# Key-value products of batches 3 to 7: two heads in the column halves of the TensorE array instead of a masked 128x128 product

## The chip, the cores and the metric

The kernel runs on one core of one Trainium2 chip. The metric is the device time of one launch in microseconds (us). Before the change, three runs gave 277.59, 277.82 and 278.0 us, a median of 277.82 us. Engines are named as in the profile: PE is TensorE's matmul, PEld its weight load, DVE is VectorE, ACT is ScalarE, POOL is GpSimd and SP is SyncE, which here only issues DMAs.

## What is computed

The kernel is a linear attention without softmax, followed by a feed-forward layer with a leaky activation:

```
kv  = einsum('bhsd,bhse->bhde', k, v)        # 64 x 64 for each batch and head
o   = einsum('bhsd,bhde->bhse', q, kv)
x   = o / sqrt(mean(o*o, -1) + 1e-6) * g_norm  # then heads side by side: 4608 x 512
h   = x @ w_in                                # 4608 x 2048
g   = max(h, 0) + alpha * min(h, 0)
out = g @ w_out                               # 4608 x 512, float32
```

There are 8 batches, 8 heads, 576 positions in each, 64 columns in each head, d_model 512 and d_ff 2048. Inputs and output are float32; the matrix products run on float16 operands and add up in float32.

## The kernel before, in words

**Windows and units.** The 4608 rows are worked in 9 windows of 512 rows (`w`). A window of the feed-forward part has 16 units (`u`), one for each block of 128 columns of the hidden layer. In unit `u` of window `w`, PE runs four matmuls with 512 moving columns into one PSUM bank (`m1_mm`, line 487; from window 3 on the first unit is cut into 384 and 128 columns, line 510), ACT and DVE turn that bank into 128 x 512 of the hidden layer (`m1_evac`, lines 494 and 498), and PE runs seven matmuls with 256 moving columns (`prod_mm`, line 665) of the product with `w_out` of window `w - 1`, which is done with 7 products of half size in place of 8. The sums for that are DVE's (`s_sum`, lines 603 to 609), and so are most of the reads of the finished sums (`y_read`, lines 697 to 709).

**Attention between the units.** After these matmuls, the call `attention(w + 1, u)` puts a piece of the next window's attention into the same unit. The order of the instructions of every engine is the order of the program (a manual schedule on all five engines), so the tables `ATT_ROW`, `QT_AT`, `REG_AT` and `REG_2` say in which unit a piece is issued. For windows 3 to 8 the pieces are these:

- `kv`: `row_kv` calls `step_kv` for each of the four pairs of heads. Heads 2j and 2j+1 are loaded side by side, so `k` and `v` of a pair have 128 columns. Five matmuls (four runs of 128 rows and one rest, lines 351 to 358) add up the 128x128 product of the whole pair in PSUM. Its two diagonal blocks of 64x64 are the products that are wanted; the other two blocks mix two heads. DVE's `tensor_mul` with `mask32` (line 360) writes the tile `kv_sb` in float16, with zeros in the mixed blocks. Pairs 0 and 2 use the PSUM bank with tag `s`, pairs 1 and 3 one of the two with tag `o`. Two pairs are issued in unit 0 and two in unit 1 (in units 2 and 3 for batch 3).
- `mm`: `rows_mm` multiplies 128 rows of `q` (transposed, in `qt_sb`) with `kv_sb` of the four pairs, with 128 moving columns (lines 429, 435 and 439), and ACT squares the result (line 444). It comes in units 2, 4, 6 and 8 (4, 5, 7 and 9 for window 3), the third time into the bank with tag `s`.
- `ssq`, `rs`, `norm`: DVE's sums (line 450), ACT's root (line 459), DVE's product (line 467), and a transposing DMA that SP issues.

**Loads.** POOL issues loads that cast to float16 (`load_gated`). `k` of a later batch lands in `kst` with the heads outermost, and ACT copies it pair by pair to `ksb` (`regroup_pair`, line 177): in units 9, 11, 13 and 15 of the window before (`REG_AT`), for batch 3 in units 0, 0, 1 and 2 of window 2 (`REG_2`). `v` is read by the matmuls as it landed (`vst`, the rest in `vsb`).

Batches 0 to 2 make their products with `step_kv` too, at other places: batch 0 in the start phase, batches 1 and 2 during windows 0 and 1.

Of the kernel before, what the change touches and what calls it, by code (L numbers as in the profile page):

```python
# [9 lines left out]
FP32 = mybir.dt.float32  # L10
FP16 = mybir.dt.float16
# [6 lines left out]
def kernel(  # L18
# [11 lines left out]
    nc = tc.nc  # L30

    B, H, S, D = q.shape
# [3 lines left out]
    P = 128  # L36
    NPAIR = H // 2
    W = 512
# [15 lines left out]
    const_p = ctx.enter_context(tc.tile_pool(name="constp", bufs=1))  # L54
# [4 lines left out]
    attn_p = ctx.enter_context(tc.tile_pool(name="attn", bufs=2))  # L59
# [6 lines left out]
    ps_s = ctx.enter_context(tc.tile_pool(name="pss", bufs=1, space=bass.MemoryType.PSUM))  # L66
# [10 lines left out]
    def early_pair(eng, nm, tag):  # L77
# [14 lines left out]
            name=nc.get_next_instruction_name(),  # L92
# [9 lines left out]
    mask32 = const_p.tile([P, P], FP32, name="mask32")  # L102
# [8 lines left out]
    qt_sb = [const_p.tile([P, NPAIR, PAD + S + PAD], FP16, name=f"qt_sb{i}") for i in range(2)]  # L111
# [6 lines left out]
    for r in range(P // D):  # L118
        nc.sync.dma_start(
            out=alpha_row[NF : NF + 1, r * D : (r + 1) * D], in_=g_norm[:].unsqueeze(0)  # L120
# [7 lines left out]
    for i in range(NBUF):  # L128
        t = {}
# [34 lines left out]
    def buf_of(b, nm):  # L164
        return bufs[min(b, B_NAT) % 2 if nm == "q" else b % NBUF][nm]
# [38 lines left out]
    def regroup_pair(b, nm, j):  # L204
        regroup(b, nm, 2 * j, 2 * j + 2, nc.scalar)
# [76 lines left out]


    qts, kvs, xts = {}, {}, {}

    def rows(b):
        return P0 if b == 0 else P

    def n_runs(b):
        return T0 if b == 0 else NT  # L290

    def pair_cols(b, nm, j):
        def f(t):
            n = rows(b)
            if nm == "v" and b == 0:
                h = 2 * j % HH
                return stages[b, nm, 2 * j // HH][0:n, h : h + 2, t, :]
            if nm == "v" and t < TPP:
                return stages[b, nm][:, 2 * j : 2 * j + 2, t, :]
            if nm == "v":  # L300
                return buf_of(b, nm)[0:n, 0, 2 * j : 2 * j + 2, :]
            return buf_of(b, nm)[0:n, t, 2 * j : 2 * j + 2, :]
        return f
# [33 lines left out]
    def dma_t(b, ts=tuple(range(NT))):  # L337
        qt = qt_sb[b % 2][:, :, PAD : PAD + S]
        for t in ts:
            c0, c1 = t * P, min((t + 1) * P, S)  # L340
            src = stages[b, "q"][:, t] if t < TPP else buf_of(b, "q")[0:REM, TPP]
            nc.sync.dma_start_transpose(
                out=qt[:, :, c0:c1], in_=src.rearrange("p h d -> p (h d)"),
            )
        for j in range(NPAIR):
            qts[b, j] = qt_sb[b % 2][:, j, PAD : PAD + S]

    def step_kv(b, j, pool=(ps_s, "s")):
        ks, vs = pair_cols(b, "k", j), pair_cols(b, "v", j)
        kv_ps = pool[0].tile([P, P], FP32, name="kv_ps", tag=pool[1])  # L350
        for t in range(n_runs(b)):
            nc.tensor.matmul(  # L352
                out=kv_ps[:],
                lhsT=ks(t),
                rhs=vs(t),
                start=(t == 0),
                stop=(t == n_runs(b) - 1),
            )
        kvs[b, j] = attn_p.tile([P, P], FP16, name="kv_sb", tag=f"kv{j}")
        nc.vector.tensor_mul(out=kvs[b, j][:], in0=kv_ps[:], in1=mask32[:])  # L360


    ots = {}
# [1 line left out]
    def step_ot(w, j, pool=None, parts=1):  # L365
        if pool is not None:
            ot_ps = pool[0].tile([P, W], FP32, name="ot_ps", tag=pool[1])
        else:
            ot_ps = ps_o.tile([P, W], FP32, name="ot_ps", tag="o")
        n0 = w * W  # L370
        while n0 < (w + 1) * W:
            b = n0 // S
            n1 = min((b + 1) * S, (w + 1) * W, n0 + W // parts)
            nc.tensor.matmul(  # L374
                out=ot_ps[:, n0 - w * W : n1 - w * W], lhsT=kvs[b, j][:],
                rhs=qts[b, j][:, n0 - b * S : n1 - b * S], start=True, stop=True,
            )
            n0 = n1
        sq = attn_p.tile([P, W], FP16, name="sq_sb")
        for c in col_parts(parts):  # L380
            nc.scalar.activation(out=sq[:, c], in_=ot_ps[:, c], func=AF.Square)
        ots[w, j] = (ot_ps, sq)

    def col_parts(parts):
        n = W // parts
        return [slice(i * n, (i + 1) * n) for i in range(parts)]
# [33 lines left out]
    def rows_mm(w, i):  # L420
        n0 = w * W + i * P
        b, r = divmod(n0, S)
        pool, tag = (ps_s, "s") if i == 2 else (ps_o, "o")
        o_ps = pool.tile([P, W], FP32, name="or_ps", tag=tag)
        for j in range(NPAIR):
            cols = o_ps[:, j * P : (j + 1) * P]
            if r + P <= S:
                c = PAD + r
                nc.tensor.matmul(  # L429
                    out=cols, lhsT=qt_sb[b % 2][:, j, c : c + P], rhs=kvs[b, j][:],  # L430
                    start=True, stop=True,
                )
            else:
                assert r + PAD == S
                nc.tensor.matmul(
                    out=cols, lhsT=qt_sb[b % 2][:, j, S : S + P], rhs=kvs[b, j][:],
                    start=True, stop=False,
                )
                nc.tensor.matmul(
                    out=cols, lhsT=qt_sb[(b + 1) % 2][:, j, 0:P], rhs=kvs[b + 1, j][:],  # L440
                    start=False, stop=True,
                )
        sq = attn_p.tile([P, W], FP16, name="sq_sb")
        nc.scalar.activation(out=sq[:], in_=o_ps[:], func=AF.Square)  # L444
        ots[w, "r", i] = (o_ps, sq)
# [291 lines left out]
    Q_POOL, S_POOL, O_POOL = (ps_q, "q"), (ps_s, "s"), (ps_o, "o")  # L737
# [7 lines left out]
    def h_at(i):  # L745
# [7 lines left out]
        out=alpha_ps[:], lhsT=alpha_row[0 : NF + 1, 0:P], rhs=ident[0 : NF + 1, 0 : NF + 1],  # L753
# [6 lines left out]
        out=beta_sb[:], in0=alpha_ps[:, 0:NF], scalar1=-1.0, scalar2=1.0, op0=ALU.mult, op1=ALU.add,  # L760
    )
    keep_warm(2)
    step_kv(0, 0)
    keep_warm(1)
    step_ot(0, 0)
    regroup0("q", 1)
    keep_warm(1)
    step_t(0, 1, h_at(1))
    regroup0("k", 1)
    ssq_mm(0, 0)  # L770
    keep_warm(1)
    step_kv(0, 1, h_at(2))
    keep_warm(1)
    step_ot(0, 1)
    regroup0("q", 2, 2)
    keep_warm(1)
# [20 lines left out]
    first = [ps_h.tile([P, W], FP32, name="h_ps", tag="h1")]  # L797
# [170 lines left out]
            ATT_1.setdefault(at, []).append((what, j))  # L968
    ATT = {"t": step_t, "kv": step_kv, "ot": step_ot, "ssq": step_ssq}

    def row_kv(w, j):
        step_kv(w, j, O_POOL if j % 2 else S_POOL)

    ATT_ROW = {}
    for first, kv_at, d in ((True, (2, 2, 3, 3), 1), (False, (0, 0, 1, 1), 0)):
        at_row = {}
        for what, ats in (
            ("kv", kv_at), ("mm", (2 + d, 4, 6, 8)), ("ssq", (4, 6, 8, 10)),
            ("rs", (5, 7, 9, 11)), ("norm", (5, 7, 9, 11)),
        ):  # L980
            for j, at in enumerate(ats):
                at_row.setdefault(at if what == "kv" else at + d, []).append((what, j))
        ATT_ROW[first] = at_row
    ROWS = {"kv": row_kv, "mm": rows_mm, "ssq": rows_ssq, "rs": rows_rs, "norm": rows_norm}
    QT_AT = {False: {7: (0,), 9: (1,), 11: (2, 3, 4)}, True: {8: (0,), 10: (1,), 12: (2, 3, 4)}}

    def attention(w, u):
        if W_ROW <= w < NW:
            for what, j in ATT_ROW[w == W_ROW].get(u, ()):
                if what != "kv" or w < B:  # L990
                    ROWS[what](w, j)
            if w + 1 < B:
                dma_t(w + 1, QT_AT[w == W_ROW].get(u, ()))
        elif w < NW:
            for what, j in (ATT_1 if w == 2 else ATT_AT).get(u, ()):
                if what == "t" and w >= B_NAT:
                    continue
                if w < B or what in ("ot", "ssq"):
                    if w == 2 and what in ("kv", "ssq"):
                        pool = Q_POOL if j % 2 == 0 else S_POOL  # L1000
                        (step_kv if what == "kv" else step_ssq)(w, j, pool)
                    else:
                        ATT[what](w, j)
# [1 line left out]
    REG_AT = {9 + 2 * j: (("k", j),) for j in range(NPAIR)}  # L1005

    Y3_AT = [(13, 13), (13, 13), (13, 13), (13, 14), (14, 14), (14, 15), (15, 15), (15, 15), (15, 15), (15, 15), (15, 15), (15, 15), (15, 15), (15, 15), (15, 16), (16, 16)]
    REG_2 = {0: (("k", 0), ("k", 1)), 1: (("k", 2),), 2: (("k", 3),)}

    for w in range(1, NW):  # L1010
        if w + 2 < B:
            load_gated(w + 2)
        for u in range(NF):
# [45 lines left out]
            if w == 2:  # L1059
                for nm, j in REG_2.get(u, ()):  # L1060
                    regroup_pair(3, nm, j)
    w = NW - 1
# [16 lines left out]
    for h in range(2):  # L1079
        half = slice(h * P, (h + 1) * P)  # L1080
        for n, i in Y_LIST[-NK:]:
# [3 lines left out]
            out=y_sb[:, 1, half], in0=ybank[w, "Z", 1 + h][:, half], in1=part[w, "u2"][:, 1, half]  # L1085
# [33 lines left out]
```

## Time and profile before

| what | value |
|---|---|
| median of three runs | 277.82 us (277.59 to 278.0) |
| profiled execution: span from its first to its last instruction | 275.2 us |
| what lies around the span (277.82 less 275.2) | 2.6 us |
| granted TensorE clock, mean | 1.000 |
| PE busy | 269.1 us, 1973 matmuls |
| PEld busy | 176.1 us, 1973 weight loads |
| DVE busy | 231.2 us, 451 instructions |
| ACT busy | 154.9 us, 286 instructions |
| POOL busy | 86.3 us, 123 instructions |

The profiled execution is known by its span; the difference to the median stands for what lies before its first and after its last instruction. A line of a group gives the source line, engine, operation, tiles and shapes, how often it ran, then busy time and the mean of one in ns, then idle time before it. Matmuls are pipelined: a matmul is shown as busy until its last result is out, so consecutive ones overlap in the records, and the time that one takes from the engine is the distance to the start of the next. The chain of work that ended last is therefore the better view of PE; its pieces give start, length and count.

### The profile page before, as it was taken

To read this page: it belongs to the slowest core of one execution; us is meant where nothing else is said; L and a number is where in the kernel's file an instruction comes from. 1 tells how busy PE (TensorE), PEld (TensorE's weight loads), DVE (VectorE), ACT (ScalarE), POOL (GpSimd) and SP (SyncE) were. 2 spreads that over 40 slices of the span, in tenths; PEclk is the share of its full clock that TensorE was granted. 3 is DMA by queue.
4 is the path that set the end of the run, shared out by engine and by line. 5 is a ranking of instruction groups with operands and counts; after the bars stand their busy time and mean duration, and the time that the engine had idled before them with its cause. 6 is when DMAs were issued, how large, how long until landed. Compare 5 with 4: busy or idle time off the path is not lost.

```text
span 275.2 us, 5282 instructions
## 1 busy us (share of the span) xinstructions
PE 269.1 (98%) x1973; PEld 176.1 (64%) x1973; DVE 231.2 (84%) x451; ACT 154.9 (56%) x286; POOL 86.3 (31%) x123
## 2 busy tenths in 40 slices
PE   7899999999999999999999999999999999999995
PEld 3454454555776776676667766676667666666794
DVE  6659758799789979997999799978997999887863
ACT  3568446799989746644665456645545553444210
POOL 8853463660912338127322641100111011000200
PEclk9999999999999999999999999999999999999999
DMA  8999999999999849997984799520322032201223
GB/s 160 197 203 198 197 202 189 215 132 182 129 172 129 124 91 138 174 204 100 173 155 120 114 166 175 118 87 2 76 76 79 6 83 67 76 2 38 72 84 114
DMA packets 87341, 34.53 MB, mean 125 GB/s; under 512 B 58884, under 2 KB 85652, under 8 KB 87316
## 3 DMA queue, kind: packets, MB, share of 16 engines
q0 software_dynamic: 58064, 24.35, 68.3%
q1 hardware_dynamic: 28212, 8.83, 16.9%
q10 hardware_dynamic: 1040, 1.02, 1.2%
q8 instruction: 15, 0.25, 0.4%
q14 instruction: 10, 0.08, 0.1%
HBM read 36.71 MB, written 9.44 MB: 168 GB/s over the span
## 4 chain that ended last, share of the span: by engine, by line
PE 87%; DMA 10%; POOL 1%; issue 1%; DVE 0%; POOLq 0%
PE h_ps L487 38%; PE yY L665 15%; PE yX L665 10%; PE yZ L665 10%; DMA qst<-in_q_dram 8%; PE y L519 4%; PE kv_ps L352 3%; DMA w_in_sb<-in_moe_w_in_dram 2%; PE h_ps L510 2%; PE or_ps L429 2%; PE qt_ps L308 1%; PE ssq_ps L397 1%; PE yZ L660 1%; PE ot_ps L374 1%; POOL vst L142 0%
## 5 line engine op out<-in xcount | busy, mean ns | idle before, releaser
L487 PE MATMUL h_ps<-xt,w_in_sb 128*128 128x512 f16 x544 | 136.8, 379 | 0.0
L494 ACT ACTIVATE m_sb<-h_ps 128x512 f32<-128x512 f32 x144 | 86.1, 598 | 79.8 <-PE h_ps L487 69.6
L498 DVE SCALAR_TENSOR_TENSOR gt<-m_sb,beta_sb,h_ps 128x512 f16<-128x512 f32 x144 | 106.4, 745 | 23.6 <-ACT m_sb L494 21.8
L487 PEld LDWEIGHTS <-w_in_sb 128*128 128x128 f16 x544 | 51.6, 98 | 38.9
L530 POOL DMA_DIRECT2D out_dram<-y_sb x36 | 22.6, 630 | 134.8 <-DVE y_sb L709 43.7
L665 PEld LDWEIGHTS <-s 128*128 128x128 f16 x496 | 48.5, 98 | 19.1
L665 PEld LDWEIGHTS <-gt 128*128 128x128 f16 x384 | 37.3, 98 | 14.0
L665 PE MATMUL yY<-wsum,s 128*128 128x256 f16 x256 | 36.3, 273 | 0.0
L665 PE MATMUL yX<-w_out_sb,gt 128*128 128x256 f16 x256 | 36.1, 273 | 0.0
L159 POOL DMA_DIRECT2D qst<-in_q_dram x20 | 17.7, 923 | 1.8 <-DMA vst<-in_v_dram 1.8
L665 PE MATMUL yY<-wsum,gt 128*128 128x256 f16 x128 | 17.6, 273 | 0.0
L444 ACT ACTIVATE sq_sb<-or_ps 128x512 f16<-128x512 f32 x24 | 14.3, 597 | 5.7 <-PE or_ps L429 4.6
L665 PE MATMUL yZ<-wsum,s 128*128 128x256 f16 x120 | 16.7, 273 | 0.0
L665 PE MATMUL yZ<-w_out_sb,s 128*128 128x256 f16 x120 | 16.7, 273 | 0.0
L467 DVE TENSOR_TENSOR x_rows<-or_ps,rstd_r 128x512 f16<-128x512 f32 x24 | 16.4, 685 | 0.0
L450 DVE TENSOR_REDUCE ssq_r<-sq_sb 128x8 f32<-128x512 f16 x24 | 16.3, 680 | 0.0
L519 PE MATMUL y<-w_out_sb,gt 128*128 128x512 f16 x64 | 15.9, 379 | 0.0
L605 DVE TENSOR_TENSOR s<-s,gt 128x512 f16<-128x512 f16 x32 | 13.5, 422 | 0.5
L603 DVE TENSOR_TENSOR s<-gt 128x512 f16<-128x512 f16 x32 | 13.5, 420 | 0.0
L609 DVE TENSOR_TENSOR s<-gt,s 128x512 f16<-128x512 f16 x32 | 13.3, 420 | 0.0
L697 DVE TENSOR_TENSOR u<-yY,p 128x512 f32<-128x512 f32 x16 | 11.0, 684 | 1.9 <-PE yY L665 1.7
L607 DVE TENSOR_TENSOR s<-gt 128x512 f16<-128x512 f16 x32 | 12.6, 418 | 0.0
(88 smaller groups left out, 269.9 us busy)
## 6 DMA issues: line engine op xcount, KB each, us to landing
out_dram<-y_sb POOLq DMA_DIRECT2D x16, 256.0 KB, 2.7
kst<-in_k_dram POOLq DMA_DIRECT2D x7, 512.0 KB, 7.0
vst<-in_v_dram POOLq DMA_DIRECT2D x6, 512.0 KB, 9.2
qst<-in_q_dram POOLq DMA_DIRECT2D x20, 128.0 KB, 6.8
w_out_sb<-in_moe_w_out_dram POOLq DMA_DIRECT2D x8, 256.0 KB, 11.6
out_dram<-y_sb SPq DMA_DIRECT2D x5, 256.0 KB, 2.3
w_in_sb<-in_moe_w_in_dram POOLq DMA_DIRECT2D x2, 512.0 KB, 10.6
qst<-in_q_dram POOLq DMA_DIRECT2D x2, 512.0 KB, 12.2
```

What stands on the lines that cost most here:

```text
L159: nc.gpsimd.dma_start(out=st[:, t, :, :], in_=srcs["q"][b, :, t * P : (t + 1) * P, :].rearrange("h p d -> p h d"),)
L444: nc.scalar.activation(out=sq[:], in_=o_ps[:], func=AF.Square)
L450: nc.vector.tensor_reduce(out=ssq[:], in_=sq[:].rearrange("p (h d) -> p h d", h=H), axis=mybir.AxisListType.X, op=ALU.add,)
L467: nc.vector.tensor_tensor(out=xr[:], in0=o_ps[:].rearrange("p (h d) -> p h d", h=H), in1=rstd[:].unsqueeze(2).to_broadcast([P, H, D]), op= ...
L487: nc.tensor.matmul(out=h_ps[:], lhsT=w_in_blk(c, g), rhs=xts[w][:, c, :], start=(c == 0), stop=(c == NC - 1),)
L494: nc.scalar.activation(out=m_sb[:], in_=h_ps[:], func=AF.Relu, scale=-1.0)
L498: nc.vector.scalar_tensor_tensor(out=gts[w, i][:, r, :], in0=m_sb[:], scalar=beta_sb[:, g : g + 1], in1=h_ps[:], op0=ALU.mult, op1=ALU.add,)
L519: nc.tensor.matmul(out=y[:], lhsT=gt_cols(w, g, a * P, (a + 1) * P), rhs=w_out_blk(g), start=(g == 0), stop=(g == NF - 1),)
L530: engs[store_turn[0] % len(engs)].dma_start(out=dst, in_=src)
L603: nc.vector.tensor_add(out=t[:], in0=a21, in1=a22)
L605: nc.vector.tensor_sub(out=t[:], in0=sums[w, 1, k][:], in1=a11)
L665: nc.tensor.matmul(out=bank, lhsT=lhs, rhs=rhs, start=fresh, stop=(c == NK - 1), skip_group_check=True,)
```

## The change

For batches 3 to 7, `row_kv` makes the products for each head by itself. The stationary operand is the 64 columns of `k` of one head, the moving operand the 64 columns of `v` of the same head. The even head's result goes to PSUM partitions 0 to 63 and the odd head's to partitions 64 to 127, so the two heads of a pair use the two column halves of the array, and their matmuls alternate. All four pairs share one PSUM tile of 128 x 256 in the bank with tag `s`. Two DVE copies, of 64 partitions x 256 elements each, move the diagonal blocks to float16. The results of a batch lie in one of two constant tiles `kv_masked`; `step_kv`, which batches 0 to 2 still use, writes all of its 128x128 there, zeros in the mixed blocks included, and later batches write only the diagonal blocks. All four pairs are issued in unit 0 (unit 2 for batch 3), and for batch 3 the copy of `k` of pair 3 moves from unit 2 to unit 1.

```diff
+    kv_masked = [const_p.tile([P, NPAIR, P], FP16, name=f"kv_masked{i}") for i in range(2)]
...
-        kvs[b, j] = attn_p.tile([P, P], FP16, name="kv_sb", tag=f"kv{j}")
-        nc.vector.tensor_mul(out=kvs[b, j][:], in0=kv_ps[:], in1=mask32[:])
+        kvs[b, j] = kv_masked[b % 2][:, j, :]
+        nc.vector.tensor_mul(out=kvs[b, j], in0=kv_ps[:], in1=mask32[:])
...
-    def row_kv(w, j):
-        step_kv(w, j, O_POOL if j % 2 else S_POOL)
+    def row_kv(b):
+        kv_ps = ps_s.tile([P, NPAIR, D], FP32, name="kv_ps", tag="s")
+        for j in range(NPAIR):
+            ks, vs = pair_cols(b, "k", j), pair_cols(b, "v", j)
+            for t in range(n_runs(b)):
+                for i in range(2):
+                    rows_i = slice(i * D, (i + 1) * D)
+                    nc.tensor.matmul(
+                        out=kv_ps[rows_i, j, :], lhsT=ks(t)[:, i, :], rhs=vs(t)[:, i, :],
+                        start=(t == 0), stop=(t == n_runs(b) - 1), skip_group_check=True,
+                    )
+        for i in range(2):
+            rows_i = slice(i * D, (i + 1) * D)
+            nc.vector.tensor_copy(
+                out=kv_masked[b % 2][rows_i, :, rows_i], in_=kv_ps[rows_i, :, :]
+            )
+        for j in range(NPAIR):
+            kvs[b, j] = kv_masked[b % 2][:, j, :]
...
-    for first, kv_at, d in ((True, (2, 2, 3, 3), 1), (False, (0, 0, 1, 1), 0)):
-        at_row = {}
+    for first, kv_at, d in ((True, 2, 1), (False, 0, 0)):
+        at_row = {kv_at: [("kv", None)]}
...
-    REG_2 = {0: (("k", 0), ("k", 1)), 1: (("k", 2),), 2: (("k", 3),)}
+    REG_2 = {0: (("k", 0), ("k", 1)), 1: (("k", 2), ("k", 3))}
```

The uses of `kvs[b, j]` in `step_ot` and `rows_mm` change only in that they take the slice as it is.

More of the change, by code (lines that the diff above doesn't have):

```diff
@@ L374, in step_ot @@
             nc.tensor.matmul(
-                out=ot_ps[:, n0 - w * W : n1 - w * W], lhsT=kvs[b, j][:],
+                out=ot_ps[:, n0 - w * W : n1 - w * W], lhsT=kvs[b, j],
                 rhs=qts[b, j][:, n0 - b * S : n1 - b * S], start=True, stop=True,
@@ L429, in rows_mm @@
                 nc.tensor.matmul(
-                    out=cols, lhsT=qt_sb[b % 2][:, j, c : c + P], rhs=kvs[b, j][:],
+                    out=cols, lhsT=qt_sb[b % 2][:, j, c : c + P], rhs=kvs[b, j],
                     start=True, stop=True,
@@ L435, in rows_mm @@
                 nc.tensor.matmul(
-                    out=cols, lhsT=qt_sb[b % 2][:, j, S : S + P], rhs=kvs[b, j][:],
+                    out=cols, lhsT=qt_sb[b % 2][:, j, S : S + P], rhs=kvs[b, j],
                     start=True, stop=False,
@@ L439, in rows_mm @@
                 nc.tensor.matmul(
-                    out=cols, lhsT=qt_sb[(b + 1) % 2][:, j, 0:P], rhs=kvs[b + 1, j][:],
+                    out=cols, lhsT=qt_sb[(b + 1) % 2][:, j, 0:P], rhs=kvs[b + 1, j],
                     start=False, stop=True,
@@ L969 @@
     ATT = {"t": step_t, "kv": step_kv, "ot": step_ot, "ssq": step_ssq}
-    def row_kv(w, j):
-        step_kv(w, j, O_POOL if j % 2 else S_POOL)
+    def row_kv(b):
[16 more added lines that the diff above has]
+            kvs[b, j] = kv_masked[b % 2][:, j, :]
     ATT_ROW = {}
-    for first, kv_at, d in ((True, (2, 2, 3, 3), 1), (False, (0, 0, 1, 1), 0)):
-        at_row = {}
+    for first, kv_at, d in ((True, 2, 1), (False, 0, 0)):
+        at_row = {kv_at: [("kv", None)]}
         for what, ats in (
-            ("kv", kv_at), ("mm", (2 + d, 4, 6, 8)), ("ssq", (4, 6, 8, 10)),
+            ("mm", (2 + d, 4, 6, 8)), ("ssq", (4, 6, 8, 10)),
             ("rs", (5, 7, 9, 11)), ("norm", (5, 7, 9, 11)),
@@ L981 @@
             for j, at in enumerate(ats):
-                at_row.setdefault(at if what == "kv" else at + d, []).append((what, j))
+                at_row.setdefault(at + d, []).append((what, j))
         ATT_ROW[first] = at_row
-    ROWS = {"kv": row_kv, "mm": rows_mm, "ssq": rows_ssq, "rs": rows_rs, "norm": rows_norm}
+    ROWS = {"mm": rows_mm, "ssq": rows_ssq, "rs": rows_rs, "norm": rows_norm}
     QT_AT = {False: {7: (0,), 9: (1,), 11: (2, 3, 4)}, True: {8: (0,), 10: (1,), 12: (2, 3, 4)}}
@@ L989, in attention @@
             for what, j in ATT_ROW[w == W_ROW].get(u, ()):
-                if what != "kv" or w < B:
+                if what != "kv":
                     ROWS[what](w, j)
+                elif w < B:
+                    row_kv(w)
             if w + 1 < B:
```

## The prediction

> **What bounds the kernel now.** I read the busy table first, then the chain of work that ended last, then that chain in the windows around the key-value products, because a mean over the whole span can't say what one stage is limited by.
>
> ```profile
> PE 269.1 (98%) x1973; PEld 176.1 (64%) x1973; DVE 231.2 (84%) x451; ACT 154.9 (56%) x286; POOL 86.3 (31%) x123
> ...
> PE 87%; DMA 10%; POOL 1%; issue 1%; DVE 0%; POOLq 0%
> ```
>
> PE is busy for 98% and holds 87% of the chain; the DMA part lies in the first 32 us, before batch 3 is touched. Matmul records overlap, so "98% busy" alone doesn't show that PE is full. The chain in order of time does (start, length, piece, number of matmuls), here around the products of batch 5 and, after the dots, of batch 6:
>
> ```profile
> 123.31 0.33 PE yX L665 x3
> 123.64 0.56 PE kv_ps L352 x10
> 124.20 0.86 PE h_ps L487 x4
> 125.06 0.76 PE yX L665 x7
> 125.83 0.56 PE kv_ps L352 x10
> 126.39 0.86 PE h_ps L487 x4
> ...
> 151.93 0.56 PE kv_ps L352 x10
> ```
>
> Each piece begins where the last one ends, and no other engine stands between. A unit is 0.86 + 0.77 = 1.63 us, 16 of them 26.06; with two kv pieces of 0.56 and four or_ps pieces of 0.22 a window should take 28.06 us. The kv blocks of batches 4 and 5 start at 95.58 and 123.64: 28.06 apart. From 123.64 to 151.93 it is 28.29, and there one or_ps piece is of eight matmuls, 0.22 more. So in these windows PE's stream of columns is the time, to the hundredth, and whatever the kv blocks gain or lose on PE goes into the total one for one.
>
> **The price of a matmul by its width.** Distances in the chain: 0.216 us at 512 columns (0.86 / 4), 0.1094 at 256 (1.75 for 16), 0.0556 at 128:
>
> ```profile
> 266.61 0.87 PE yZ L665 x8
> 267.49 0.89 PE yZ L660 x16
> ```
>
> That is 0.418 ns a column and 2 ns more. At 64 columns it makes 28.9 ns. The trace has 64-column matmuls (ot_ps, line 374) only in front of one of 448 columns; the two take 0.22 us together, as one of 512 does, so 64 columns with a weight load of their own cost their share there.
>
> **The change on PE.** It removes 20 matmuls of 128 columns per batch, 1.11 us, and adds 40 of 64 columns and 40 weight loads of 64 columns. Five batches have 5.56 us at stake, 2.0% of the span. The trace has no matmul on half of the array, so three things are unknown.
>
> (a) *Do the two halves run beside each other?* If so, 20 pairs at 28.9 ns take 0.58 us, 0.53 less. If one follows the other, 40 at 28.9 are 1.16, which is 0.05 more. These are the ends. I take the first: the two heads of a pair use different columns of the array, different output partitions and different operands, and nothing in the program orders them.
>
> (b) *Do the loads keep up?* A load is recorded with 98 ns, but loads overlap:
>
> ```profile
> 11.44 0.28 PEld L308 LDWEIGHTS <-qsb 96*128 96x128 f16 x6 [0.55 <-DVE qsb L199]
> ...
> 11.45 0.43 PE L308 MATMUL qt_ps<-ident,qsb 96*128 96x96 f16 x6
> ```
>
> Six loads of 128 columns in 0.28 us: (0.28 - 0.098) / 5 = 36 ns apart, under matmuls (0.43 - 0.21) / 5 = 44 ns apart. That is the densest that the trace shows, and the matmuls may set it, so it is an upper bound for a full load. A half load should then cost between nothing and 36 ns of PE's time; an estimate of 18 ns, half the columns at that pace, would be covered by matmuls run singly and nearly by pairs (2 x 18 against 29). I take nothing, since the 64-column matmuls above showed none; the outer end, a load that nothing hides, is the recorded 98 ns. If half loads follow each other at 36 ns, a block takes 40 x 0.036 = 1.44 us, 0.33 more than now.
>
> [...]
>
> (c) *What does going to halves and back cost?* Twice a batch. At most the pipeline runs empty: a 128-column matmul is recorded with 219 ns and the next normally starts after 56, so 0.163 us each. At least nothing. The nearest row is the one change of shape in the trace, the 17-row transposition of line 752:
>
> ```profile
> 5.85 0.66 PE L308 MATMUL qt_ps<-ident,qsb 96*128 96x96 f16 x6
> 6.44 0.28 PE L752 MATMUL alpha_ps<-ident,y_sb 17*128 17x17 f32 x1
> 6.66 0.83 PE L277 MATMUL warm_ps<-y_sb 128*128 128x512 f16 x2
> ```
>
> The six before it stand (0.66 - 0.28) / 5 = 76 ns apart, so the seventh was due about 6.31 and came at 6.44, before the six were out (6.51): 0.13 us late, at half the later pace (76 against 44 ns). I halve it: 0.07 us a change, 0.13 a block. [...]
>
> Block: 0.58 + 0.13 = 0.71 us in place of 1.11: 0.40 less, five times 2.0 us.
>
> **DVE.** Removed: four products of 128 columns, 286 ns each, 1.14 us. Added: two copies of 256 elements a partition. No such copy is in the trace; the nearest rows are
>
> ```profile
> L360 DVE TENSOR_TENSOR kv_sb<-kv_ps,mask 128x128 f16<-128x128 f32 x32 | 8.1, 286 | 3.4 <-PE kv_ps L352 3.4
> ...
> L713 DVE TENSOR_TENSOR y_sb<-yZ,u 128x256 f32<-128x256 f32 x2 | 0.8, 422 | 0.2 <-PE yZ L665 0.2
> ```
>
> so 286 to 422 ns each, 0.84 us by the upper: 0.3 a batch less. None of it is on the path. They queue ahead of the next gt (line 498): around batch 6 the products start at 153.24 and the next gt at 154.01, so 0.84 pushes it back by 0.07, and its bank is wanted one unit later. The reader of the new products is or_ps, two units on at the earliest. Were that cover gone, 0.1 a batch. Over a window DVE is busy for 25.5 of 28.1 us; with PE at 27.7 it stays under.
>
> **Order.** All four pairs now need `k` in unit 0. ACT's last copy (line 177) ran 150.06 to 150.67 and the block starts at 151.76: covered by 1.1 us. For batch 3 the copy of pair 3 moves from 72.04 to behind the one at 69.96, so to about 70.5 to 71.1, while the block starts at 70.56 and reaches pair 3 at 71.0: up to 0.1 us, once, and the m_sb queued behind it starts 0.5 later, one unit before its bank is wanted. No DMA is issued at another place in its queue; `v` comes free one unit earlier, which no load in these windows waits for. The shared bank `s` is next wanted by or_ps three units later; the banks `o` lose a user.
>
> **Sum.** 5 x 0.40 - 0.1 = 1.9 us off the span of 275.2, so 273.3, and with the 2.6 us around it (277.82 - 275.2) 275.9 us.
>
> **Rivals.** *Loads set the pace* (slower). Place: the 40 loads of a block. It decides as soon as half loads can't be hidden, follow each other and take over 28 ns (1.11 / 40). At 36 ns: 5 x 0.33 = +1.65, 279.5 us; with two full drains of 0.163 a block +1.6 more, 281.1. At 98 ns, nothing hidden, 5 x 2.8 = +14, 292. For it: twice the loads for half the time. Against: loads took 64% of PE's time and matmuls never waited for one in the windows.
> *The changes of shape eat the gain.* At 0.163 and with the first load of each side not hidden (0.098) a change costs 0.26, a block 0.58 + 0.52 = 1.10: no change, 277.8. Drains alone: 0.91, 276.8.
> *The change does not do what it says*: the halves follow each other. 1.16 + 0.13 a block, +0.9 us, 278.7; without a price for the changes of shape 278.1.
> *DVE takes the bound*: against it the 2.6 us that it idles in each window, against 0.4 that PE gives back.
>
> **How the numbers follow.** Pairs beside each other, loads hidden, price of the change of shape 0 to 0.163: 275.2 to 276.9, 0.50. Gain eaten or halves in turn without further price: 277.3 to 278.4, 0.16. Loads or halves in turn with a price: 278.4 to 281.1, 0.31, two thirds of it below 280; beyond 281.1, 0.03. Measurements of this kernel can tell about 0.2%, 0.56 us, from no change. Faster by more 0.51, within 0.15, slower by more 0.34. The range from 275.0 to 280.0 leaves out about 0.14. The likeliest case by itself is 275.2 to 276.9.
>
> **What would show it.** Right: the kv piece of the chain is one of 40 matmuls and 0.6 to 0.9 us long, windows are 27.7 us apart, the pieces on both sides touch it, DVE shows two copies below 0.43. Wrong: starts of kv matmuls 36 ns or more apart with loads back to back, a gap ahead of and behind the block, idle PE in the units after it, or a wait of kv for ksb in the window of batch 3.

## The result and the profile after

The changed kernel takes 276.48 us (median of 14 runs, 275.96 to 277.03) against 277.56 us for the kernel before beside it (14 runs, 276.63 to 278.0). The ratio is 0.9962, with a 95% interval of 0.9952 to 0.9971: 1.05 us faster, where 1.9 us were forecast.

The busy table of after comes first, then its chain of work (start, length, piece, number of matmuls) around the products of batches 4 and 5.

```profile
PE 267.8 (97%) x2073; PEld 173.5 (63%) x2073; DVE 230.8 (84%) x441; ACT 154.9 (56%) x286; POOL 87.0 (32%) x123
```

```profile
96.54 0.75 PE kv_ps L979 x40
...
124.01 0.33 PE yX L666 x3
124.34 0.75 PE kv_ps L979 x40
125.09 0.97 PE h_ps L488 x4
126.06 0.77 PE yX L666 x7
```

The 40 matmuls are one piece of 0.75 us in place of two of 0.56. But the four matmuls behind it take 0.97 in place of 0.86: 0.11 us are lost there, and the chain counts them to the next piece. So a block costs 0.75 + 0.11 = 0.86 against 1.11. The starts of the blocks confirm it: 96.54 to 124.34 is 27.80 us, where it was 28.06. Still no other engine stands in the chain here.

The span is 275.1 us, hardly less than the 275.2 of before, and this needs care. The first block of batch 3 starts at 71.49 in this execution and at 70.56 in that of before, 0.93 us later, and the delay comes from loads in the start phase: the two longest pieces that wait for q took 6.66 and 15.04 us against 6.05 and 14.73. In five other executions of kernels that are the same up to there it starts at 71.26 (even heads only), 70.85 (halves in turn), 70.64 (thirty-two moving columns), 70.88 (whole pairs) and 71.09 (the changed kernel again), so the start phase by itself varies by some 0.6 us from execution to execution. From the first block to the end it is 203.6 us (275.1 - 71.49) against 204.6 (275.2 - 70.56): 1.0 us less, which is what the runs show. This execution was the slowest of the 14.

Something else takes a little of the gain. In the first unit of window 4 the second group of four h_ps matmuls takes 0.32 us in this execution and 0.22 in that of before, so PE is 0.10 late there. In the profile of the same kernel run again (last experiment) it is 0.22 late at this place, and the chain names the wait, a transposing DMA that lands at 95.51:

```profile
91.90 3.61 DMA xt<-x_rows
...
95.55 0.38 PE h_ps L511 x4
```

None of the other eleven profiles shows it. Whether the change has a part in it isn't shown.

One instruction level down, these are after's matmuls around the block, then its weight loads:

```profile
123.85 0.49 PE L666 MATMUL yX<-w_out_sb,gt 128*128 128x256 f16 x3
124.27 0.32 PE L979 MATMUL kv_ps<-vst,ksb 128*64 128x64 f16 x8
124.42 0.20 PE L979 MATMUL kv_ps<-vsb,ksb 128*64 128x64 f16 x2
124.45 0.29 PE L979 MATMUL kv_ps<-vst,ksb 128*64 128x64 f16 x8
...
125.02 1.04 PE L488 MATMUL h_ps<-xt,w_in_sb 128*128 128x512 f16 x4
```

```profile
124.27 0.71 PEld L979 LDWEIGHTS <-ksb 128*64 128x64 f16 x40 [0.21 <-issue]
125.02 0.55 PEld L488 LDWEIGHTS <-w_in_sb 128*128 128x128 f16 x4
```

The last of the three yX matmuls started at 123.85 + 0.49 - 0.273 = 124.07; the next was due 0.109 later, at 124.18, and came at 124.27: **0.09 us late**. Behind the block it is the same: the last pair started at 124.90 (0.626 after the first, by the starts in the trace), the next matmul was due 0.03 later and came at 125.02, again 0.09 late. In both places the first load starts together with its matmul, after the load engine stood idle for 0.21 us ("issue": it waited for nothing that the profile shows). Inside the block, two matmuls of a pair start 3 to 4 ns apart, and two of the same half 31.7 ns apart; only the second pair of a block starts later, 53 ns after the first.

These 0.09 us have one form in all these kernels. From matmul to matmul on the whole array the next starts 0.163 us before the recorded end of the last in these windows. Where the shape changes, in every kernel here that has halves or quarters, it starts 0.067 to 0.071 us before that end, whether the last matmul had 32, 64, 256 or 512 moving columns; 0.163 - 0.07 is the 0.09 that is lost. The load of the new shape starts no earlier, even where the load engine had been idle for 0.42 us, as at batch 2 in the version of the changed kernel that comes last below (53.66 + 0.38 - 0.07 = 53.97):

```profile
53.66 0.38 PE L520 MATMUL y<-w_out_sb,gt 128*128 128x512 f16 x1
...
53.97 0.71 PEld L979 LDWEIGHTS <-ksb 128*64 128x64 f16 x40 [0.42 <-issue]
```

The profile models the ends of matmuls, so it doesn't show whether the array is empty at that moment.

### The profile page after: what moved, and what is told of

Read it like the earlier page. It is cut to its first block, busy times and chain, and to the rows that moved or that the text cites. A ratio compares the mean times of both kernels' runs of the same rounds, so it can differ in the third digit from the quotient of the medians.

```text
span 275.1 us, 5472 instructions
## 1 busy us (share of the span) xinstructions
PE 267.8 (97%) x2073; PEld 173.5 (63%) x2073; DVE 230.8 (84%) x441; ACT 154.9 (56%) x286; POOL 87.0 (32%) x123
## 4 chain that ended last, share of the span: by engine, by line
PE 87%; DMA 10%; POOL 1%; issue 1%; DVE 0%; POOLq 0%
PE h_ps L488 38%; PE yY L666 15%; PE yX L666 10%; PE yZ L666 10%; DMA qst<-in_q_dram 8%; PE y L520 4%; DMA w_in_sb<-in_moe_w_in_dram 2%; PE h_ps L511 2%; PE or_ps L430 2%; PE kv_ps L979 1%; PE qt_ps L309 1%; PE kv_ps L353 1%; PE ssq_ps L398 1%; PE yZ L661 1%; PE ot_ps L375 1%
```

## The experiments

All ran beside the kernel before, and each ratio is to that. The theory was that the halves run beside each other and that the shape changes eat part of the gain.

**Even heads only.** The products of the odd heads and their copy are left out.

```diff
-                for i in range(2):
+                for i in range(1):
```

> Leaves out the products of the odd heads of batches 3 to 7 and their copy: 20 matmuls on one half only. Theory: the odd heads ran beside the even ones, so leaving them out saves almost nothing: 20 x 0.029 + 0.2 = 0.78 us a block against 0.85, about 0.4 us off the total, 276.1. Rival (16 ns each whichever half): 20 x 0.016 + 0.2 = 0.52, five times 0.33: 1.7 us off, 274.8.

Measured: 276.27 us, ratio 0.9960 (0.9947 to 0.9974). The chain of this kernel at the same block:

```profile
124.02 0.75 PE kv_ps L979 x20
124.76 0.97 PE h_ps L488 x4
```

Twenty matmuls take the same 0.75 us as forty. The odd heads cost nothing beside the even ones, and the rival with 16 ns a matmul falls: it asked for 0.32 us and the edges. But a matmul alone on its half came every 32 ns too, not every 29 as estimated, so the 0.4 us that I expected to save didn't come.

**Halves in turn.**

```diff
-            for t in range(n_runs(b)):
-                for i in range(2):
+            for i in range(2):
+                for t in range(n_runs(b)):
```

> Same 40 matmuls and 40 loads as after, but the five of the even head of a pair come first, then the five of the odd head, so that neighbours nearly always use the same half of the array. Theory (two halves run beside each other, a pair in 32 ns, plus about 0.1 us at each change of shape): without neighbours in the other half a matmul costs its own stream, 28.9 ns, so a block takes 40 x 0.029 + 0.2 = 1.36 us against 0.85 after, five times 0.5: about 2.5 us slower than after, 279.0, slower than before. Rival (a 64-column matmul simply costs 16 ns, whichever half it uses): the block stays at 0.85 and the time at 276.5.

Measured: 276.54 us, ratio 0.9968 (0.9957 to 0.9979), so no slower than after. The piece is 0.81 us long. Read by itself this would speak for the rival, which the experiment above has ruled out. The matmuls of this kernel show what happened; `vst` is read by the first four runs of a head, `vsb` by its fifth:

```profile
123.65 0.34 PE L979 MATMUL kv_ps<-vst,ksb 128*64 128x64 f16 x7
123.80 0.20 PE L979 MATMUL kv_ps<-vsb,ksb 128*64 128x64 f16 x1
123.83 0.20 PE L979 MATMUL kv_ps<-vst,ksb 128*64 128x64 f16 x2
123.86 0.20 PE L979 MATMUL kv_ps<-vsb,ksb 128*64 128x64 f16 x1
```

Seven matmuls on `vst` started before the even head's fifth, the one on `vsb`; only four of them belong to the even head. Three of the odd head, which come later in the program, were started ahead of it. So in this kernel these three didn't wait for an older matmul of the other half, the starts weren't in the program's order, and that order hardly mattered (0.81 against 0.75 us). My expectation had taken a strict order for granted. The theory's 279.0 us was wrong by that, and the rival's 276.5 came out for another reason than its own.

**Thirty-two moving columns.** Half of the columns of v are left out; loads as in after.

```diff
-                        out=kv_ps[rows_i, j, :], lhsT=ks(t)[:, i, :], rhs=vs(t)[:, i, :],
+                        out=kv_ps[rows_i, j, 0:32], lhsT=ks(t)[:, i, :], rhs=vs(t)[:, i, 0:32],
```

> Leaves out half of the columns of v: the 40 matmuls have 32 moving columns in place of 64, with the same 40 loads. If the stream of columns sets the 32 ns of a pair, a pair should fall to about 32 x 0.418 + 2 + 3 = 18 ns, a block by 20 x 0.0135 = 0.27 us, the total by 1.3 us to 275.1. If the loads set it (two half loads of 16 ns in turn), block and time stay: 0.75 us for the kv piece, 276.5.

Measured: 276.02 us, ratio 0.9957 (0.9943 to 0.9971), not told apart from after's 0.9962. The chain decides it:

```profile
123.38 0.74 PE kv_ps L979 x40
124.11 0.97 PE h_ps L488 x4
```

Half the stream, and the piece is 0.74 us. So the stream of columns didn't set the pace here. Nor did two loads in turn, of 16 ns each, as I had put it: then the even heads alone would have been faster.

**Whole array, thirty-two moving columns**, and **quarters**. The first loads 128 columns and streams 32 columns of each pair's v, the second loads 32 columns and streams 32; the rest of each product is left out.

```diff
+                    out=kv_ps[:, j, 0:32], lhsT=ks(t), rhs=vs(t)[:, 0, 0:32],
```

> Leaves out all but 32 columns of v of each pair: 20 matmuls on the whole array with 128-column loads and 32 moving columns. This asks what the 32 ns between two matmuls of the same half are. If every load and matmul on the same part of the array take 32 ns at least, the kv piece is 20 x 0.032 = 0.64 us with nothing late around it: 5 x 0.47 below before, 275.1. If it is the half load that is slow and full loads are faster, the pace follows the stream, 15 ns, and the piece is 0.3 to 0.4 us: 5 x 0.75 below before, 273.8.

```diff
+                        out=kv_ps[i * D : i * D + 32, j, 0:32], lhsT=ks(t)[:, i, 0:32], rhs=vs(t)[:, i, 0:32],
```

> Leaves out three quarters of each product: loads of 32 columns and 32 moving columns, in the column quarters 0 and 2 of the array, 40 matmuls alternating as in after. Two matmuls of the same half came 31.7 ns apart with 64 and with 32 moving columns, and 25 ns apart on the whole array with 32 moving columns. If the columns of the load set the 31.7 ns, half the columns bring it to the stream or the 25 ns seen on the whole array: kv piece 0.6 us or less, 0.7 us less in total than after. If it is a fixed time of a load and a matmul on a part of the array, the piece stays at 0.74.

Measured: 275.51 us, ratio 0.9919 (0.9907 to 0.9932), and 275.67 us, ratio 0.9937 (0.9920 to 0.9954). Two chains, whole array first:

```profile
123.05 0.49 PE kv_ps L977 x20
123.54 0.87 PE h_ps L488 x4
```

```profile
123.84 0.60 PE kv_ps L979 x40
124.44 0.97 PE h_ps L488 x4
```

The first piece lies between the two that I had written down (0.64, or 0.3 to 0.4 us), the second is as asked for if the columns of the load set the pace. On the whole array the matmuls come every 0.49 / 20 = 25 ns and nothing is late behind them; in quarters a pair comes every 25 ns as well, by the starts in the trace, and the 0.11 us are lost again. With the stream the same 32 columns in three kernels, the distance is 25 ns behind a load of 32 columns, 31.7 behind one of 64, and 25 behind one of 128 on the whole array. **The 31.7 ns came with the half load, not with the stream**: fewer moving columns didn't shorten them, fewer columns of the load did (on a smaller part of the array), and behind a full load with twice the columns the distance was 25. So here the half load was slower than the full one. What sets the 25 ns, the same behind two different loads, isn't shown. The records of single loads agree, from the groups of after:

```profile
L979 PEld LDWEIGHTS <-ksb 128*64 128x64 f16 x200 | 3.6, 112 | 1.2 <-issue 1.1
...
L353 PEld LDWEIGHTS <-ksb 128*128 128x128 f16 x40 | 2.7, 98 | 0.9
```

A load of 64 columns is recorded with 112 ns, one of 128 with 98. In the whole-array kernel the first load of the block began 0.11 us ahead of its matmul (122.78 and 122.89); where the shape changes it began together with it.

**Two units.** Pairs 0 and 1 in unit 0, pairs 2 and 3 in unit 1, the copies after the second part.

```diff
-        at_row = {kv_at: [("kv", None)]}
+        at_row = {kv_at: [("kv", 0)], kv_at + 1: [("kv", 1)]}
```

> The block is cut in two: pairs 0 and 1 in unit 0, pairs 2 and 3 in unit 1 (units 2 and 3 for batch 3), one PSUM tile, the two copies after the second part. That adds two changes of shape per batch and nothing else. Theory (a change costs 0.09 to 0.11 us): 0.2 x 5 = 1.0 us slower than after, less 0.16 since batch 3 no longer waits for the copy of k of pair 3: 277.3, hardly faster than before. Rival (the time around the block is paid once by something else, such as the first load of the next group): no more than 0.2 us from after.

Measured: 277.36 us, ratio 0.9994 (0.9984 to 1.0004). The chain of this kernel:

```profile
124.25 0.43 PE kv_ps L983 x20
124.69 0.97 PE h_ps L488 x4
125.65 0.77 PE yX L666 x7
126.42 0.43 PE kv_ps L983 x20
126.85 0.97 PE h_ps L488 x4
```

Two pieces of 0.43 cost 0.11 more than one of 0.75, and there are two of 0.97 in place of one: 0.22 us a batch for two more changes of shape (0.09 at each, and one more second pair that starts 0.02 late), 1.1 in five, less the 0.16 at batch 3. The runs show 0.88 (277.36 - 276.48). Cut in two, the change gains nothing that can be measured.

**Whole pairs at the new place.** All of the change but the halves.

```diff
+                    out=kv_ps[:, j, :], lhsT=ks(t), rhs=vs(t),
```

> Everything of the change but the halves: 20 matmuls of 128 columns on the whole array, in one PSUM tile, all in unit 0, two copies of the diagonal blocks, the same two constant tiles. Theory (the gain is PE's, from the halves alone): the kv piece is 1.11 us and nothing is late around it, so the time is that of before, 277.5. Rival (the place, the single bank or DVE's two copies in place of four products bring part of it): at least 0.3 us below before.

Measured: 277.40 us, ratio 0.9994 (0.9984 to 1.0004). Its chain has one piece of 1.12 us, with nothing late behind it:

```profile
123.97 1.12 PE kv_ps L977 x20
125.09 0.86 PE h_ps L488 x4
```

The place, the single bank and DVE's two copies bring nothing that can be measured; the gain comes from the halves.

**Batch 3 and batch 2.** In after the block of batch 3 is 0.94 us long, not 0.75: pair 2 ends at 71.92, and pair 3 starts at 72.08, just after ACT's copy of its k (70.90 to 72.03). Three kernels went after this gap, two of them with batch 2 by halves as well.

```diff
-    for first, kv_at, d in ((True, 2, 1), (False, 0, 0)):
+    for first, kv_at, d in ((True, 3, 1), (False, 0, 0)):
...
-        ("t", (0, 2, 3, 8)), ("kv", (5, 5, 7, 7)), ("ot", (7, 7, 11, 12)), ("ssq", (8, 9, 12, 13))
+        ("t", (0, 2, 3, 8)), ("kv", (5,)), ("ot", (7, 7, 11, 12)), ("ssq", (8, 9, 12, 13))
```

> After with one edit: batch 3's block in unit 3 in place of 2, the copy of k of pair 3 back in unit 2. Theory: the 0.16 us gap in front of pair 3 goes, the piece of batch 3 falls from 0.94 to 0.75 us, the total by 0.2 to 276.3, which the runs can hardly tell; the trace can. Rival (the gap is not the wait for the copy): the piece stays at 0.94.

> The version that the runs point to: batch 3 a unit later, and batch 2 by halves as well (all four pairs in unit 5 of window 1, bank q, two copies). Theory: 0.2 us from the first, 1.11 - 0.86 = 0.25 from the second, 0.45 less than after: 276.0. Rival (window 1 has less slack, and the single bank makes the sums of squares wait for the copies): no gain over after, or a gap of PE in unit 5 to 8 of window 1.

> The version with batch 2 by halves and batch 3 a unit later, but the copy of k of pair 3 stays in unit 1 as in after (moving it back to unit 2 took the slack away again). Theory (the gap in batch 3's block is the wait for that copy): the piece of batch 3 falls to 0.75 us, the whole to 1.0 us or more below before times one: 0.3 to 0.4 us below after, 276.1. Rival (the gap is something else): the piece stays near 0.9.

The first: 276.46 us, ratio 0.9951 (0.9938 to 0.9964), and its piece is still 0.89 us: with the block I had also moved the copy, which now ended at 72.90, while pair 3 started at 72.95. The wait moved along. The second: 276.23 us, ratio 0.9944 (0.9932 to 0.9956), the same gap. The third leaves the copy in unit 1. Its chain at batches 2 and 3:

```profile
54.04 0.75 PE kv_ps L979 x40
...
72.65 0.75 PE kv_ps L979 x40
```

Both blocks have 0.75 us and the gap is gone, so it was the wait for the copy. But batch 2 gains less than its block does: a sum of squares in window 1 is late, as the rival of the second version had it. Here it is in this kernel and, after the dots, in after:

```profile
63.83 0.38 PE ssq_ps L398
...
64.43 0.23 PE ssq_ps L398
```

PE is 0.17 us late at 63.83, just after ACT's squares, which ran 63.18 to 63.77; the second version has the same, and after hasn't. It stands in unit 13 and not in units 5 to 8, which the rival had named, and what makes the squares late isn't shown. From the block of batch 2 to the first yX piece behind it, it is 12.97 us (54.04 to 67.01) against 13.07 in after (54.40 to 67.47): 0.10 less, where 0.25 were expected. The time is 276.20 us, ratio 0.9948 (0.9931 to 0.9966). The changed kernel beside it:

> The changed kernel itself, beside the two others on the same chip: 0.9962 of before, some 1.05 us below it.

It took 276.75 us, ratio 0.9967 (0.9953 to 0.9982). The two intervals overlap: the traces show 0.10 us less on PE at batch 2 and 0.19 at batch 3, some 0.3 in all, and the runs don't establish that the version is faster than after.

## Why the prediction was right, and where it was too large

**What bounds the kernel** held. PE's stream is still the time in these windows, and what the block gave back on PE came off the total: 4 x 0.26 us for batches 4 to 7 (27.80 against 28.06 between blocks) and 0.06 for batch 3 (0.94 + 0.11 against 1.11) are 1.10 us, and the runs show 1.05. In the two profiles of the changed kernel 0.10 and 0.22 us of that are lost again in window 4, to a wait that the prediction doesn't have.

**(a) The two halves run beside each other**: shown, by the even heads alone. The rival in which the change doesn't do what it says falls.

**(b) Loads at nothing exposed**: this term was mis-sized. Half loads weren't hidden: with a half load each, matmuls came every 31.7 ns on their half, with 32 moving columns as with 64, and not every 28.9, the estimate from the widths. Twenty pairs take 0.63 us, not 0.58: 0.06 us a batch. Had the loads also followed each other from half to half, the rival in which loads set the pace would have held with 40 x 0.032; it fell because forty half loads in two halves took the same 0.75 us as twenty in one. A half load was recorded with 112 ns, a full one with 98.

**(c) The changes of shape at 0.07**: right in kind, too small. They cost 0.09 on each side, and the late second pair 0.02 more: 0.21 a batch where I took 0.13. The row that I read held the right size. Its 17-row matmul came at 6.44, 0.07 before the six were out at 6.51, the same lead as at the changes to halves and back, and 0.163 - 0.07 is the 0.09 that was measured. The 0.13 that I read there and halved is the difference to the 0.20 by which matmuls overlap at that slower pace (0.28 - 0.076); the lead at the change is 0.07 at both paces. Nor is the full 0.163 right, which I had taken as the price if the array drains: the new matmul starts at 124.27, the old one is recorded until 124.34. What the new shape waits for, the array or its own first load, stays open; both start together at that moment. The rival in which the changes eat the gain was right about where the cost lies, and wrong about the size: it took 0.26 a change. With four changes a batch, in the block cut in two, they did eat the gain.

So the block is 0.84 to 0.86 us (0.63 + 0.21 by the starts) and not 0.71, and the saving 0.26 and not 0.40. **Order**: the wait of batch 3 for k, put at up to 0.1, was 0.16 to 0.19. **DVE**: two copies of 418 ns against 422 taken; they queue ahead of the next gt as foreseen and PE never waits for one. Five times 0.06 for the loads, five times 0.08 for the changes and up to 0.09 for batch 3 make up some 0.8 of the 0.85 us between 1.9 and 1.05.

## What to carry to other kernels

Where PE is full, two products that each use half of the array's columns did run side by side here (0.75 us for the forty matmuls of both, 0.75 for the twenty of one), but a matmul of 64 moving columns with a half load of its own came every 31.7 ns on its half, where the widths gave an estimate of 28.9, and each entry to and exit from the narrow shape cost 0.09 us. So put all narrow matmuls of a stage into one block, and count two changes of shape per block before splitting it: here the block cut in two gave the whole gain back. Test whether things run beside each other by leaving one of them out, not by reordering them, since PE started the matmuls of the two halves out of the program's order here. And to price a change of shape, look in a trace for how long before the recorded end of one shape the next one starts, and compare that with two matmuls of the same shape.

## What the runs showed of the hardware that I had not expected

Matmuls of one column half started ahead of older ones of the other half (seven on `vst` before the even head's fifth, in the kernel with the halves in turn). A load of 64 columns was slower than one of 128: 112 against 98 ns recorded, and 31.7 against 25 ns between matmuls with 32 moving columns. And no load was brought forward across a change of shape to halves or back: the first one started with its matmul (both at 124.27 in after), where in the kernel on the whole array it started 0.11 us earlier (122.78 and 122.89). Both started 0.07 us before the recorded end of the last matmul of the old shape, with 32 as with 512 moving columns of that matmul.
